# Earlier loads of the attention heads, a later chain for the outputs, and an inverse root on GpSimd

## Chip, core and metric

The kernel runs on one core of one Trainium2 chip, as one launch. The metric is the device time in microseconds, taken as the median over runs; lower is better. Engines are written as the profile has them: PE is TensorE, DVE is VectorE, ACT is ScalarE, POOL is GpSimd, SP is SyncE, which here does nothing but issue DMAs in a fixed order.

## What is computed

One transformer block on 2048 rows of 576 float32 numbers. The conditioning vector `c` gives, through SiLU and one product with `w_mod`, six rows: shift, scale and gate for each half of the block.

```python
h = layernorm(x) * (1 + ca) + sa
x = x + ga * (softmax_attention(h @ wqkv, 32 heads of 18) @ wo)
h = layernorm(x) * (1 + cb) + sb
x = x + gb * ((sigmoid(h @ w_gate) * (h @ w_up)) @ w_down)     # inner width 4608
layernorm(x) = (x - mean) / sqrt(var + 1e-5)
```

The scores' softmax runs over all 2048 keys. Products keep nearly float32 accuracy: operands are split into a high and a low part (`fp32r`), and the parts are multiplied separately.

## The kernel before

**Three stages.** First the rows are normalized, transposed and projected to q, k and v; the split parts of q and k go to DRAM (`qd`, `kd`). Then attention runs in 32 units of 16 steps. Last, the gated block runs with a Strassen-like scheme of seven products for each of 18 column blocks, twice (two halves of the rows).

**A unit of attention** is two heads and half of the queries. Units 0 to 15 take the first half of the queries, units 16 to 31 the second. A step `kt` (0 to 15) takes 128 keys: four score matmuls (line 916), four exponentials on ACT (line 920), and the product of earlier probabilities with v (`values`, line 539, two steps late, so that a pair of steps holds two groups of eight such matmul records). Beside them runs `maxima`, six steps and more ahead: it computes the scores of the next unit but one turned the other way (line 446) and takes their row maxima on DVE (line 452). At the end of a unit's maxima, which falls at step 9 of the unit before it, DVE makes `nm`, `turned` and `parts` (lines 464 to 469, the last two instructions are a cast and a subtraction of 128x32 in SBUF), and SP sends them through DRAM into rows of the q tile (lines 470 and 475). Most units pair two of the maxima's tiles by a ReLU on ACT; the units in `SINGLE` (0, 1, 16, 17, 18, 27, 28, 29) don't.

**Order of work.** During attention the order on PE, DVE and SP is the order of the program (`manual_schedule`); ACT and POOL follow a scheduler's order. A string of letters says what a step does: `t` scores, `m` one turn of the maxima, `v` values, `k` copies a finished unit's output out of PSUM (`taken`, the copy is `oT`, line 553), and `w` does one piece of side work. `k` and `w` are in odd steps alone. Each `w` takes the next entry of the list that `outputs` returned and the next piece of a generator: `first_rows` from step 240 (`FROM0`) on, `project_o(8, 16)` from `FROM1` on.

**`load_heads(u + 2)`** issues eight DMAs on SP that fetch q and k of the unit after next (1.5 MB, line 413 to 421). Before, it stands behind step 1 of unit u.

**`outputs`** divides a finished unit by its sums: `gather` (line 571) moves the sums across partitions by a DMA, `spread` takes the reciprocal on DVE (line 574), writes it to DRAM (`rows_r`, line 575) and reads it back broadcast (line 576); `scaled` multiplies and splits on POOL (lines 579 to 581, three instructions of 128x512); `stored` writes the result to `od` in DRAM (line 592). The list has one entry for each `w`, that is for steps 1, 3, 5 and so on of the next unit.

**`first_rows`** scales `wo` (`load_wo`, ending in a row of empty yields that wait for unit 15's outputs), multiplies the first eight row tiles with it (`project_o(0, 8)`), normalizes the result and makes the operands of the last stage. `load_o(t)` fetches row tile t of `od` (the tile `t`, lines 645 and 650) and the row of x (line 652). `project_o` calls it one tile ahead; a tile takes two `w` (line 676). Row tiles 8 to 15 go the same way in units 27 to 29.

**`ln_scales_steps`** turns variances into inverse roots: `var + 1e-5` on DVE (line 167), the root on ACT (line 169), then reciprocal and one Newton step on DVE (lines 172 to 177). It is called four times ahead of attention, once in attention (in unit 20, eight columns), and twice in the last stage. Between its yields `first_rows` puts one more.

Of the kernel before, what the change touches and what calls it, by code (L numbers as in the profile page):

```python
# [15 lines left out]
F32 = mybir.dt.float32  # L16
F32R = mybir.dt.float32r
AF = mybir.ActivationFunctionType
ALU = mybir.AluOpType
# [4 lines left out]
P = 128  # L24
# [10 lines left out]
EPS = 1e-5  # L35
# [2 lines left out]
HW = S // 2  # L38
UNITS = H
LEAD = 6  # L40
FROM0, FROM1 = 15 * 16, 27 * 16 + 13
DL = 384
ORDER = (1, 6, 2, 7, 5, 4, 3)
LOOK = 3
# [11 lines left out]
def tile_block(ctx, tc, x_in, wqkv, wo, w_gate, w_up, w_down, c_in, w_mod, out):  # L56
    nc = tc.nc
# [3 lines left out]
    const = ctx.enter_context(tc.tile_pool(name="const", bufs=1))  # L61
# [4 lines left out]

    ident = const.tile([P, P], F32, name="ident")
    make_identity(nc, ident)
    eps = const.tile([P, 1], F32, name="eps")
    nc.vector.memset(eps, EPS)  # L70
    mcol = const.tile([P, 2, 5], F32, name="mcol")
    mcol2 = const.tile([P, 2, 6], F32, name="mcol2")
    gb_b = const.tile([P, D], F32, name="gb_b")
# [85 lines left out]
    def ln_scales(pool, mv, rs):  # L159
        for _ in ln_scales_steps(pool, mv, rs):  # L160
            pass

    def ln_scales_steps(pool, mv, rs):

        n = rs.shape[-1]
        var = pool.tile([P, n], F32, name="var")
        nc.vector.tensor_scalar_add(var, mv[:, :, 1], EPS)
        sd = pool.tile([P, n], F32, name="sd")
        nc.scalar.activation(sd, var, AF.Sqrt)
        yield  # L170
        r0 = pool.tile([P, n], F32, name="r0")
        nc.vector.reciprocal(r0, sd)

        nc.vector.tensor_mul(sd, r0, r0)
        nc.vector.tensor_mul(sd, sd, var)
        nc.vector.tensor_scalar(sd, sd, -0.5, 1.5, op0=ALU.mult, op1=ALU.add)
        nc.vector.tensor_mul(rs, r0, sd)

    def ln_apply(z, xt, mean, rs):

# [208 lines left out]
    def temp(shape, dtype):  # L389
        temps["n"] += 1  # L390
        return qpool.tile(shape, dtype, name=f"t{temps['n'] % 2}")
# [8 lines left out]
    def heads(u):  # L400
        return qsets[u % 3], ksets[u if u < 2 else 2 + (u - 2) % 3]

    def load_heads(u):


        qs, ks = heads(u)
        half, p = divmod(u, H // 2)
        n = S if u < 2 else S + 512
        own = slice(half * HW, (half + 1) * HW)
        for h in range(2):  # L410
            rows = slice((2 * p + h) * DH, (2 * p + h + 1) * DH)
            two, one = (slice(64 * h + a, 64 * h + b) for a, b in ((0, 2 * DH), (2 * DH, 3 * DH)))
            nc.sync.dma_start(
                qs[two, :].bitcast(F32), qd[:, rows, own].rearrange("l f n -> f l n").bitcast(F32)
            )
            nc.sync.dma_start(qs[one, :].bitcast(F32), qd[0, rows, own].bitcast(F32))
            nc.sync.dma_start(
                ks[two, 0:n].bitcast(F32),
                kd[0, rows, 0:n].unsqueeze(1).to_broadcast([DH, 2, n]).bitcast(F32),
            )  # L420
            nc.sync.dma_start(ks[one, 0:n].bitcast(F32), kd[1, rows, 0:n].bitcast(F32))
# [72 lines left out]
    with tc.tile_pool(name="wv1", bufs=1) as wvp:  # L494
        tiles = [[(o + D * w, P)] for o in (128, 256, 384) for w in (0, 1)] + [[(DM, 64), (D + DM, 64)]]
        for i, parts in enumerate(tiles):
# [5 lines left out]
            for g in range(2):  # L502
                pl = project_qk([(wt, 2 * g), (wt, 2 * g + 1)], run if i else None)
                col, n = parts[-1]
# [43 lines left out]
    def taken():  # L548

        if "whole" in state:  # L550
            half, p, acc = state.pop("whole")
            oT = epool.tile([P, 512], F32, name="oT")
            nc.scalar.copy(oT, acc)
            todo_out.extend(outputs(half, p, oT))
# [3 lines left out]
    def outputs(half, p, oT):  # L558


        at = turns["out"] = (turns["out"] + 1) % 3
        if state["room"] is None:
            full, hi, lo = (ppool.tile([P, 512], F32, name=f"p{i}") for i in range(3))
        else:
            room = state["room"][:, 1536 * at : 1536 * (at + 1)]
            full, hi, lo = (room[:, 512 * i : 512 * (i + 1)] for i in range(3))
            parts = room[:, 512:1536]
        sums, rec = (epool.tile([P, 16], F32, name=n) for n in ("sums", "rec"))

        def gather():  # L570
            nc.sync.dma_start(sums, oT[DH::32, :].rearrange("j (q e) -> j q e", e=16))

        def spread():
            nc.vector.reciprocal(rec, sums)
            nc.sync.dma_start(rows_r.rearrange("j (q e) -> (j q) e", e=16), rec)
            nc.sync.dma_start(full, rows_r.unsqueeze(1).to_broadcast([4, 32, 512]))

        def scaled():
            nc.gpsimd.tensor_mul(full, full, oT)
            nc.gpsimd.tensor_copy(hi.bitcast(F32R), full)  # L580
            nc.gpsimd.tensor_sub(lo.bitcast(F32R), full, hi)

        def stored():
            for h in range(2):
                f0 = (2 * p + h) * DH
                for c in range(2):
                    q, q0 = 32 * (2 * h + c), half * HW + c * 512
                    if state["room"] is None:
                        for l, part in enumerate((hi, lo)):
                            nc.sync.dma_start(od[l, f0 : f0 + DH, q0 : q0 + 512].bitcast(F32), part[q : q + DH])  # L590
                        continue
                    nc.sync.dma_start(
                        od[:, f0 : f0 + DH, q0 : q0 + 512].rearrange("l f q -> f l q").bitcast(F32),
                        parts[q : q + DH].rearrange("f (l q) -> f l q", l=2),
                    )

        return [gather, spread, None, None, scaled, None, stored]

# [3 lines left out]
    def load_wo():  # L604

        wo_h = slots.tile([P, 4, 640], F32R, name="w0")[:, :, 0:D]
        wo_l = slots.tile([P, 4, 640], F32R, name="w1")[:, :, 0:D]
        we = bgp.tile([P, 2, D], F32R, name="we")
        raws = {}

        def load(t):
            raw = raws[t] = temp([P, 2048], F32)[:, 0:D]
            if t < 4:
                paced(nc.gpsimd.dma_start(raw, wo[t * P : (t + 1) * P, :]))
            else:
                for p0 in (0, 64):
                    paced(nc.gpsimd.dma_start(raw[p0 : p0 + 64], wo[DM:D, :]))

        load(0)
        yield  # L620
        load(1)
        yield
        for t in range(5):
            raw = raws[t]
            nc.gpsimd.tensor_mul(raw, raw, ga_b)
            wh, wl = (wo_h[:, t, :], wo_l[:, t, :]) if t < 4 else (we[:, 0, :], we[:, 1, :])
            nc.gpsimd.tensor_copy(wh, raw)
            nc.gpsimd.tensor_sub(wl, raw, wh.bitcast(F32))
            if t >= 3:
                for i, w in enumerate((wh, wl)):  # L630
                    nc.gpsimd.dma_start(wod[:, i, t - 3, :].bitcast(F32), w.bitcast(F32))
            if t < 3:
                load(t + 2)
            yield
        weights.extend((wo_h, wo_l, we))
        for _ in range(8):
            yield

    def load_o(t):
# [104 lines left out]

    def first_rows():
        yield from load_wo()
        yield from project_o(0, 8)
        for t in range(8):
            ln_stats(bgp, Oa[:, t, :], mv2[:, t, :])
            yield  # L750
        for _ in ln_scales_steps(bgp, mv2[:, 0:8, :], rs2[:, 0:8]):
            yield
            yield
# [49 lines left out]
    def paced(load):  # L803

        tc.add_manual_dep(
            load.ins, state["exp"].ins.name,
            mybir.DependencyInfo(mybir.DependencyClass.Sync, mybir.DependencyReason.DATA),
            reason="paced by the steps of attention",
        )
# [70 lines left out]
    for u in range(UNITS):  # L880
        half, p = divmod(u, H // 2)
        qs, ks = heads(u)
        if u == UNITS - 1:
            state["room"] = temp([P, 2048], F32)
            turns["out"] = 2
        if u == H // 2:
            state["room"] = big.tile([P, 8, 640], F32, name="big").rearrange("p a b -> p (a b)")
        for kt in range(NT):
# [30 lines left out]
                    pr = probs[2 * c + h] = ppool.tile([P, 512], F32, name=f"p{2 * c + h}")  # L919
                    state["exp"] = nc.scalar.activation(pr, sT, AF.Exp, scale=SCALE)  # L920
            pending.append((half, p, kt, probs))
            if 0 < u < UNITS - 2 and kt == 1:
                load_heads(u + 2)
            if u in (1, 3):
                if kt == 2:
                    a = big.tile([P, 8, 640], F32, name="big")
# [332 lines left out]
```

## Time and profile before

| | us |
|---|---|
| median of 3 runs | 2955.37 |
| lowest and highest | 2953.96, 2956.30 |
| the profiled execution's own time | 2952.37 |
| its span, first to last instruction | 2950.6 |
| PE busy | 2848.5 (97%) |
| DVE busy | 2215.6 (75%) |
| ACT busy | 1570.4 (53%) |
| POOL busy | 684.8 (23%) |

Attention lies between about 238 and 1611 us of the span; unit u has about 40 us, more where side work is done. A line of the timeline gives the start in the span, the duration, engine, source line, operation, output and input tiles and, in brackets, how long the engine had been idle and who ended that. A line of a window gives for each engine the busy time, and the share of its full clock that TensorE was granted (PEclk).

### The profile page before, as it was taken

What the parts mean: (1) busy time and instruction counts of PE and PEld (TensorE: products, weight loads), DVE (VectorE), ACT (ScalarE), POOL (GpSimd) and SP (SyncE); (2) the same over time, 40 slices, a digit from 0 to 9 for tenths busy, and PEclk for the clock granted to TensorE, in tenths of its full rate; (3) what the DMA queues carried; (4) which work ended last, traced back from release to release, by engine and by line L of the source; (5) the groups of instructions that cost most, each with busy time, mean ns of one, the idle gap of its engine ahead of it and who ended that gap; (6) DMA issues with size and microseconds to landing.
All of it is one profiled execution on the core that took longest, in us unless ns stands there. A gap on an engine that the chain in (4) does not pass through costs nothing.

```text
span 2950.6 us, 46231 instructions
## 1 busy us (share of the span) xinstructions
PE 2848.5 (97%) x16901; PEld 1876.0 (64%) x16901; DVE 2215.6 (75%) x4047; ACT 1570.4 (53%) x2908; POOL 684.8 (23%) x793
## 2 busy tenths in 40 slices
PE   7999999999999999999999899988999999999999
PEld 6863333333344534334443788877888888888888
DVE  7278889999999789999872778878877555555555
ACT  3217889999977688898678323333333111111111
POOL 3112025455221007730103322233222100000000
PEclk9999999999999999999999999999999999999999
DMA  5343244444223312321344776677555845545443
GB/s 178 123 160 87 65 125 156 155 144 135 88 79 92 109 54 92 111 74 59 101 132 153 273 239 228 234 256 249 207 200 211 321 159 176 170 167 167 165 157 136
DMA packets 177135, 456.26 MB, mean 155 GB/s; under 512 B 36488, under 2 KB 86412, under 8 KB 164620
## 3 DMA queue, kind: packets, MB, share of 16 engines
q1 hardware_dynamic: 162140, 376.72, 38.8%
q0 software_dynamic: 14768, 76.59, 7.4%
q8 instruction: 133, 2.18, 0.3%
q14 instruction: 94, 0.77, 0.1%
HBM read 285.07 MB, written 167.91 MB: 154 GB/s over the span
## 4 chain that ended last, share of the span: by engine, by line
PE 77%; DVE 11%; DMA 4%; issue 3%; ACT 3%; SPq 1%; POOL 1%; POOLq 0%; DVEq 0%; ACTq 0%
PE o L539 15%; PE d L1055 14%; PE x L1019 12%; PE s L446 10%; PE s L916 10%; PE bg L1019 4%; PE bu L1019 4%; DVE mx L452 4%; PE s L276 4%; PE s L327 2%; ACT p L920 2%; PE s L676 2%; DVE w L1011 1%; DMA xs<-ho 1%; DMA t<-od 1%
## 5 line engine op out<-in xcount | busy, mean ns | idle before, releaser
L452 DVE TENSOR_REDUCE mx<-s 128x1 f32<-128x512 f32 x1664 | 1057.3, 684 | 130.8 <-PE s L446 109.5
L920 ACT ACTIVATE p<-s 128x512 f32<-128x512 f32 x2048 | 1064.3, 611 | 165.6 <-PE s L916 80.8
L446 PE MATMUL s<-k,q 54*128 54x512 f32 x1920 | 610.4, 451 | 14.7 <-ACT p L920 6.3
L916 PE MATMUL s<-q,k 56*128 56x512 f32 x1920 | 559.0, 429 | 11.6 <-DVE mx L452 8.0
L539 PE MATMUL o<-p,vaug 128*32 128x512 f32 x4096 | 560.4, 612 | 0.4 <-ACT p L920 0.4
L1055 PE MATMUL d<-wd,hh 128*128 128x288 f32 x2304 | 475.5, 301 | 27.9 <-DVE Oa L1059 25.7
L446 PEld LDWEIGHTS s<-k,q 54*128 54x128 f32 x1920 | 278.2, 186 | 281.7 <-ACT p L920 225.1
L916 PEld LDWEIGHTS s<-q,k 56*128 56x128 f32 x1920 | 263.5, 187 | 300.1 <-DVE mx L452 216.1
L1055 PEld LDWEIGHTS d<-wd,hh 128*128 128x128 f32 x2304 | 378.4, 191 | 44.0 <-DVE Oa L1059 33.6
L1059 DVE TENSOR_TENSOR Oa<-Oa,d 128x288 f32<-128x288 f32 x576 | 256.0, 452 | 133.3 <-PE d L1055 129.0
L1055 PE MATMUL d<-wd,hl 128*128 128x288 f32 x1152 | 343.8, 298 | 0.0
L1019 PE MATMUL x<-k,w 128*128 128x512 f32 x1008 | 244.3, 393 | 4.2 <-ACT w L1010 4.2
L1055 PEld LDWEIGHTS d<-wd,hl 128*128 128x128 f32 x1152 | 220.1, 191 | 0.0
L1019 PEld LDWEIGHTS x<-k,w 128*128 128x128 f32 x1008 | 188.8, 190 | 43.8 <-ACT w L1010 5.6
L1031 ACT ACTIVATE u<-u 128x512 f32<-128x512 f32 x72 | 45.4, 631 | 320.2 <-DVE u L1207 316.2
L539 PEld LDWEIGHTS o<-p,vaug 128*32 128x32 f32 x4096 | 84.0, 108 | 167.7 <-issue 155.8
L1028 ACT ACTIVATE sg<-x 128x512 f32<-128x512 f32 x36 | 21.6, 599 | 315.7 <-PE x L1019 315.6
L1061 POOL DMA_DIRECT2D out_dram<-Oa x16 | 8.7, 544 | 604.3 <-DVE Oa L1059 604.3
L455 ACT ACTIVATE over<-s 128x512 f32<-128x512 f32 x192 | 114.6, 597 | 37.9 <-PE s L446 32.3
L457 DVE CUSTOM_DVE_ANT_0 over<-s,over 128x512 f32<-128x512 f32 x192 | 129.4, 674 | 0.0
L1019 PE MATMUL x<-big,w 128*128 128x512 f32 x504 | 120.5, 390 | 2.2 <-issue 2.2
L1019 PE MATMUL x<-w,w 128*128 128x512 f32 x504 | 121.2, 390 | 0.0
(211 smaller groups left out, 3555.0 us busy)
## 6 DMA issues: line engine op xcount, KB each, us to landing
ws<-w SPq DMA_DIRECT2D x126, 640.0 KB
w<-ws SPq DMA_DIRECT2D x126, 640.0 KB
wd<-wds SPq DMA_DIRECT2D x36, 1152.0 KB
k<-kd SPq DMA_DIRECT2D x60, 360.0 KB
wds<-w POOLq DMA_DIRECT2D x18, 1152.0 KB, 5.5
k<-kd SPq DMA_DIRECT2D x60, 180.0 KB
w<-in_B_w_down_dram POOLq DMA_DIRECT2D x18, 576.0 KB, 5.1
q<-qd SPq DMA_DIRECT2D x64, 144.0 KB
```

What stands on the lines that cost most here:

```text
L276: nc.tensor.matmul(acc, w, hT[:, t, cols], start=n == 0, stop=n == len(ts_) - 1)
L327: nc.tensor.matmul(acc[:, 0:HALF], hT[:, k, rows], w, start=n == 0, stop=n == len(ts_) - 1,)
L446: nc.tensor.matmul(sp, qs[rows, qt * P : (qt + 1) * P], ks[rows, at * 512 : (at + 1) * 512], start=True, stop=True,)
L452: nc.vector.tensor_reduce(to, sp, axis=AX.X, op=ALU.max)
L455: nc.scalar.activation(over, sp, AF.Relu)
L457: nc.vector.tensor_tensor_reduce(out=over, in0=sp, in1=over, scale=1.0, scalar=LOWEST, op0=ALU.add, op1=ALU.max, accum_out=mx[:, h * n + q ...
L539: nc.tensor.matmul(acc[32 * j : 32 * j + 32, :], vaug[:, kt, (2 * p + h) * VW : (2 * p + h) * VW + 32], probs[2 * c + h], start=kt == 0, s ...
L916: nc.tensor.matmul(sT, ks[rows, kcols], qs[rows, c * 512 : (c + 1) * 512], start=True, stop=True)
L920: state["exp"] = nc.scalar.activation(pr, sT, AF.Exp, scale=SCALE)
L1019: nc.tensor.matmul(acc[v], w[:, v, a, :], X[s][:, b, :], start=first and n == 0, stop=n == 6, skip_group_check=not first,)
L1055: nc.tensor.matmul(acc[:, :HALF], a[:, f, rows], w[:, f, cols], start=n == 0, stop=n == 5)
L1059: nc.vector.tensor_add(Oa[:, t, cols], Oa[:, t, cols], acc[:, :HALF])
```

## The change

`load_heads(u + 2)` moves from the end of step 1 to the front of step 0 of a unit, ahead of the previous unit's `gather` on SP. `spread` is cut in two: `inverted` (reciprocal and the write to DRAM) at step 7, `spread` (the read back) at step 9; `scaled` moves from step 9 to 13, `stored` from 13 to 15. So that it still follows `stored`, `load_wo` has nine empty yields instead of eight, and `FROM1` lies two steps later. The root on ACT and the reciprocal on DVE give way to one `pow` with exponent -0.5 on POOL and two Newton steps on DVE, with a yield behind each.

```diff
-FROM0, FROM1 = 15 * 16, 27 * 16 + 13
+FROM0, FROM1 = 15 * 16, 27 * 16 + 15
...
-    eps = const.tile([P, 1], F32, name="eps")
-    nc.vector.memset(eps, EPS)
+    powers = const.tile([P, 8], F32, name="powers")
+    nc.gpsimd.memset(powers, -0.5)
...
         var = pool.tile([P, n], F32, name="var")
+        sd = pool.tile([P, n], F32, name="sd")
+        r0 = pool.tile([P, n], F32, name="r0")
         nc.vector.tensor_scalar_add(var, mv[:, :, 1], EPS)
-        sd = pool.tile([P, n], F32, name="sd")
-        nc.scalar.activation(sd, var, AF.Sqrt)
+        nc.gpsimd.tensor_tensor(r0, var, powers[:, 0:n], op=ALU.pow)
         yield
-        r0 = pool.tile([P, n], F32, name="r0")
-        nc.vector.reciprocal(r0, sd)
-
-        nc.vector.tensor_mul(sd, r0, r0)
-        nc.vector.tensor_mul(sd, sd, var)
-        nc.vector.tensor_scalar(sd, sd, -0.5, 1.5, op0=ALU.mult, op1=ALU.add)
-        nc.vector.tensor_mul(rs, r0, sd)
+        for to in (r0, rs):
+            nc.vector.tensor_mul(sd, r0, r0)
+            nc.vector.tensor_mul(sd, sd, var)
+            nc.vector.tensor_scalar(sd, sd, -0.5, 1.5, op0=ALU.mult, op1=ALU.add)
+            nc.vector.tensor_mul(to, r0, sd)
+            yield
...
-        def spread():
+        def inverted():
             nc.vector.reciprocal(rec, sums)
             nc.sync.dma_start(rows_r.rearrange("j (q e) -> (j q) e", e=16), rec)
+
+        def spread():
             nc.sync.dma_start(full, rows_r.unsqueeze(1).to_broadcast([4, 32, 512]))
...
-        return [gather, spread, None, None, scaled, None, stored]
+        return [gather, None, None, inverted, spread, None, scaled, stored]
...
-        for _ in range(8):
+        for _ in range(9):
             yield
...
         qs, ks = heads(u)
+        if 0 < u < UNITS - 2:
+            load_heads(u + 2)
...
-            if 0 < u < UNITS - 2 and kt == 1:
-                load_heads(u + 2)
```

## The prediction

> **What bounds the kernel now.** I read the page first, then PE's idle time, then the timeline around each idle stretch in attention.
>
> ```profile
> span 2950.6 us, 46231 instructions
> PE 2848.5 (97%) x16901; PEld 1876.0 (64%) x16901; DVE 2215.6 (75%) x4047; ACT 1570.4 (53%) x2908; POOL 684.8 (23%) x793
> ```
>
> PE works for 97% of the span, so only some 100 us of idle time are to be had, and a stretch in which PE waits lengthens the whole. The change takes no matmul away. It is worth what it does to single stalls of PE in attention; three of them lie where the change works.
>
> The first is the root in unit 20. ACT's rows, PE's rows and one window (PEclk, the share of its clock that TensorE was granted, is the third figure from the end):
>
> ```profile
> 1091.25 1.28 ACT L169 ACT_TABLE_LOAD   x1
> 1092.78 1.28 ACT L920 ACT_TABLE_LOAD   x1
> ...
> 1090.25 1.07 PE L539 MATMUL o<-p,vaug 128*32 128x512 f32 x8
> 1094.72 0.79 PE L916 MATMUL s<-q,k 56*128 56x512 f32 x1 [2.50 <-ACT p L920]
> 1095.44 1.94 PE L539 MATMUL o<-p,vaug 128*32 128x512 f32 x8
> 1099.74 1.66 PE L539 MATMUL o<-p,vaug 128*32 128x512 f32 x8
> 1102.45 1.06 PE L539 MATMUL o<-p,vaug 128*32 128x512 f32 x8
> ...
> 1094.70:1099.70 5.00, 4.98 (x18) 1.99 (x18) 1.33 (x3) 3.43 (x8) 0.00 (x0) 0.50 0.60 191
> ```
>
> ACT loads the root's table, computes, loads the exponential's table back: 1091.25 to 1094.06, 2.81 us in which no exponential runs. PE stands for 2.50 us, and then the granted clock is 0.50 for 5 us: the same eight records take 1.94 us instead of 1.07. The groups should start 2.71 us apart (1099.74 to 1102.45); the two intervals from 1090.25 to 1099.74 are 9.49 us, so the stall cost 9.49 - 5.42 = 4.07 us, 1.57 us more than the idle time itself.
>
> The others are in units 28 and 29, where the projection waits for its tile of outputs:
>
> ```profile
> 1440.62 1.47 PE L676 MATMUL s<-w,t 128*128 128x288 f32 x9
> 1450.88 2.60 PE L676 MATMUL s<-w,t 128*128 128x288 f32 x9 [4.35 <-DMA t<-od]
> 1459.02 1.47 PE L676 MATMUL s<-w,t 128*128 128x288 f32 x9
> 1465.14 1.45 PE L676 MATMUL s<-w,t 128*128 128x288 f32 x9
> 1505.72 2.60 PE L676 MATMUL s<-w,t 128*128 128x288 f32 x9 [3.76 <-DMA t<-od]
> ...
> 1429.52 0.79 SPq L413 DMA_DIRECT2D q<-qd  x1
> 1435.90 0.36 SPq L575 DMA_DIRECT2D rows_r<-rec  x1
> 1442.78 0.60 SPq L576 DMA_DIRECT2D big<-rows_r  x1
> 1443.47 1.02 SPq L645 DMA_DIRECT2D t<-od  x2
> ```
>
> These pieces should be 6.12 us apart (1459.02 to 1465.14); 1440.62 to 1459.02 is 18.40, an excess of 6.16 us for 4.35 us of idle time. The second, by the same surcharge of 1.8 us, cost 3.76 + 1.8 = 5.6 us. SP's rows show why: the heads' loads go out from 1429.52, the small write of the reciprocals behind them (1435.90) lands only at 1442.78, SP stands still until then, and the tile's load is issued behind that, at 1443.47, for a matmul due at about 1446.7.
>
> **The change part by part.** The root: the pair of table loads in unit 20 goes, and no other row holds ACT there, so -4.1 us. The Trainium skill, ScalarE: Activation LUTs, section on what ACT_TABLE_LOAD costs, puts every switch of a set at about 2.66 us, half of it a drain; for two switches that makes an estimate of 5.3 us saved on ACT and about 6.6 in all. The trace shows 2.81 us for both, and the sum uses that.
>
> The heads first, the chain later. In unit 17 this does harm:
>
> ```profile
> 924.76 0.39 SPq L645 DMA_DIRECT2D t<-od  x1
> 927.79 1.07 PE L539 MATMUL o<-p,vaug 128*32 128x512 f32 x8
> 932.85 1.06 PE L539 MATMUL o<-p,vaug 128*32 128x512 f32 x8
> 936.65 1.85 PE L676 MATMUL s<-w,t 128*128 128x288 f32 x12
> ```
>
> The first tile of outputs was requested at 924.76, ahead of the unit, which begins at 932.85. With the ninth empty yield its request comes at step 1, behind the heads and the gather on SP, and it is used at step 3. A pair of steps without projection takes 5.06 us there (927.79 to 932.85); the first piece, at 936.65 before, is due one pair later, at 941.7. In this queue a transfer issued behind the heads landed 13.3 us after their start (1429.52 to 1442.78). For the tile itself I take 1.2 us more, between nothing and the 7.4 us from 1443.47 to the matmul at 1450.88, where two tiles came at once; near the low end, since it is fetched beside the heads' last transfers. The heads start at about 932.3, when unit 16 has read its last scores; the tile lands 14.5 us later, at 946.8. PE stands for 5.1 us and pays the surcharge of 1.8: +6.9 us. The ends: 13.3 us gives 3.9 of idle time, +5.7; 20.7 us gives 11.3, +13.
>
> In units 28 and 29 it does good: no `spread` stands between the heads and `load_o` any more. The tile used at step 5 is requested at step 1. Two pieces of 6.12 us ahead of 1440.62 step 1 has its piece, at 1428.4; the unit begins 3.8 us before that (932.85 to 936.65), at 1424.6; the tile lands at 1439.1, 1.5 us before the piece that needs it. Both stalls go: -6.2 - 5.6 = -11.8 us.
>
> The next part is a collision. DVE's two small instructions at the end of a unit's maxima stand still while POOL works on SBUF:
>
> ```profile
> L468 DVE CAST parts<-turned 128x32 fp32r<-128x32 f32 x32 | 12.3, 384 | 1.1
> L469 DVE TENSOR_TENSOR parts<-turned,parts 128x32 fp32r<-128x32 f32 x32 | 11.4, 356 | 1.1
> 1241.82 2.61 POOL L723 TENSOR_TENSOR ho<-t,ho 32x512 fp32r<-32x512 f32 x2
> 1243.17 1.30 DVE L469 TENSOR_TENSOR parts<-turned,parts 128x32 fp32r<-128x32 f32 x1
> 1245.13 0.50 PE L916 MATMUL s<-q,k 56*128 56x512 f32 x1 [1.29 <-DVE mx L452]
> ...
> 813.29 0.24 DVE L574 RECIPROCAL rec<-sums 128x16 f32<-128x16 f32 x1
> 829.73 0.18 DVE L468 CAST parts<-turned 128x32 fp32r<-128x32 f32 x1
> 829.94 0.19 DVE L469 TENSOR_TENSOR parts<-turned,parts 128x32 fp32r<-128x32 f32 x1
> 813.26 1.07 PE L539 MATMUL o<-p,vaug 128*32 128x512 f32 x8
> 822.99 1.07 PE L539 MATMUL o<-p,vaug 128*32 128x512 f32 x8
> 821.23 0.59 SPq L576 DMA_DIRECT2D Oa<-rows_r  x1
> 826.11 1.29 POOL L579 TENSOR_TENSOR Oa<-Oa,oT 128x512 f32<-128x512 f32 x1 [36.23 <-DMA Oa<-rows_r]
> 1543.70 0.34 SPq L575 DMA_DIRECT2D rows_r<-rec  x1
> 1545.13 0.57 SPq L576 DMA_DIRECT2D big<-rows_r  x1
> ```
>
> The subtraction that takes 0.19 us alone took 1.30, until POOL's second instruction ended at 1244.43, and PE then stood for 1.29 us. Against 0.18 and 0.19 us the two groups hold (12.3 - 5.8) + (11.4 - 6.1) = 11.8 us of this now. The change places `scaled` anew in every unit. In unit 14 the reciprocal moves two pairs of steps later, 9.73 us (813.26 to 822.99), from 813.29 to 823.0; it runs 0.24 us, its write takes 1.43 to the read back in a quiet queue (1543.70 to 1545.13), and that 4.88 to the multiplication (821.23 to 826.11): `scaled` would start at 829.6, within 0.2 us of the cast at 829.73. So small a margin is a coin toss, unit by unit. All present collisions gone would be -11.8; one of 1.2 us in each of 26 units (without 17, 18, 28 and 29, where the projection gives DVE time) 31 - 11.8 = +19. I take +2: half of the units now quiet are hit, and some of the present ones go.
>
> The rule that speaks against this change is in the Trainium skill, SBUF — State Buffer, section on the two separate sides: VectorE and GpSimd share a port pair under an exclusive lock, and the loser blocks for the other's whole instruction. The rows at 1241.82 and 1243.17 agree; its result is the slower rival below.
>
> Last, the power and the longer Newton. Three DVE instructions more of at most 0.19 us are +0.5 us in unit 20, taken in full.
>
> ```profile
> 11.21 1.71 POOL L184 COPY x<-x 128x64 f32<-128x64 f32 x4 [1.62 <-DVE x L181]
> 17.73 0.77 PE L192 MATMUL s<-ident,x 128*128 128x128 f32 x5
> 1795.01 0.63 ACT L1031 ACTIVATE u<-u 128x512 f32<-128x512 f32 x1 [5.51 <-DVE u L1207]
> ```
>
> No row shows a power on POOL. Its product of 128x512 takes 1.29 us; eight columns are a 64th of that, so 1.29 us is also the price if each power costs as much as 64 products. I take that, the geometric middle of the ends: 0.19, what DVE needs for so small a tile, and 12.9, ten times my value. DVE reads it two `w`, four steps or 10.8 us (twice 5.42), later, so unit 20 hides all but the upper end; past that, the maxima queued behind the Newton step on DVE wait, and PE with them. Ahead of attention the cover is 4.8 us, from the end of POOL's copies (12.92) to PE's transposes (17.73): nothing at my value, up to +8 at the end. In the last stage ACT, behind the root's loads, waited 5.51 us for DVE anyway, so their removal brings nothing; a slow power there would hold the additions queued behind it on DVE by up to 12.9 us.
>
> Sum: -4.1 + 0.5 - 11.8 + 6.9 + 2 = -6.5 us. The profiled execution's own time is 2952.37 (span 2950.6 and 1.8 around it), 3.0 below the median of 2955.37; 2945.9 there is 2948.9 as a median.
>
> **The rivals.** *No stall in unit 17* (the tile overtakes the heads): -13.4 us, 2942. For it: no row shows a large transfer behind the heads; against: the small write at 1435.90, which didn't overtake them. *POOL's port decides*: `scaled` starts ahead of the subtraction in nearly all units, +19 instead of +2, 2966, slower; it decides from a start less than about 0.2 us behind the cast's. *The stalls of units 28 and 29 stay*, since the margin there is 1.5 us: without the -11.8, 2961; for it, the 7.4 us tile. *A slow power*, at its end of 12.9 us: +8 ahead of attention and +2 in unit 20 instead of nothing, 2959.
>
> **How the numbers follow.** Forecast 42%, no stall in unit 17 20%, POOL's port 20%, stalls stay 10%, slow power 8%. 0.2%, about what a measurement can tell here, is 5.9 us: faster is under 2949.5, slower over 2961.3. The forecast's own range is 2942 to 2956, so somewhat over half of it is faster: with the second case 0.45. Slower gets 0.14 of POOL's port, half of the stalls and some of the slow power: 0.21; the rest, 0.34, is the same. The range 2939 to 2965 leaves out the worst of POOL's port and of unit 17's upper end.
>
> **What would show it.** Right: no table load in attention; groups of line 539 in unit 20 without a gap; no idle time of line 676 in units 28 and 29; one of 4 to 6 us at step 3 of unit 17, with a clock of 0.50 behind it; lines 468 and 469 at a sum near 24 us. Wrong: that sum above 35 us, a gap of line 676 in unit 28, POOL's power above 5 us, or DVE waiting for it.

## The result, and the profile after

The changed kernel takes 2968.46 us in the median of five runs (2963.11 to 2972.41), the kernel before 2953.98 us of five (2951.38 to 2956.30): a ratio of 1.0047, 95% interval 1.0032 to 1.0061. It is 14 us slower. Forecast were 2948.9 us and at most 2965.

The head of the page after:

```profile
span 2961.2 us, 46269 instructions
PE 2851.4 (96%) x16901; PEld 1878.1 (63%) x16901; DVE 2222.5 (75%) x4067; ACT 1558.7 (53%) x2894; POOL 695.2 (23%) x801
```

The profiled execution is the fastest of the five, so it shows 10.6 us of the loss and not all of it. This table gives the span by stretches, worked out from the first value matmul (line 539) of each unit; "quiet" is the edit of e5 and e6 below, e15 and e16 are the last two experiments.

| us | before | changed | before, quiet | changed, quiet | e15 | e16 |
|---|---|---|---|---|---|---|
| to the first row | 238.0 | 245.4 | 242.6 | 244.7 | 238.9 | 240.4 |
| units 0 to 14 | 610.9 | 617.9 | 611.8 | 614.3 | 615.1 | 612.0 |
| 15, 16 | 90.5 | 83.1 | 88.7 | 82.4 | 83.7 | 84.0 |
| 17, 18 | 106.4 | 117.7 | 105.9 | 114.3 | 105.8 | 106.4 |
| 19, 20 | 92.0 | 87.5 | 93.6 | 85.6 | 86.5 | 86.2 |
| 21 to 27 | 293.3 | 295.0 | 287.5 | 289.5 | 289.1 | 288.1 |
| 28, 29 | 107.6 | 98.1 | 108.1 | 96.0 | 96.2 | 96.0 |
| 30, 31 | 68.5 | 75.8 | 68.5 | 76.3 | 68.5 | 68.5 |
| behind attention | 1343.6 | 1340.8 | 1338.3 | 1344.2 | 1341.7 | 1341.6 |
| span | 2950.6 | 2961.2 | 2945.0 | 2947.3 | 2925.5 | 2923.1 |

**What came as forecast.** In the changed kernel's timeline the tiles of units 28 and 29 are there when they are due (no brackets, so no idle time), and in unit 17 PE stands for 4.85 us (5.1 forecast), with a granted clock of 0.50 in the window behind it. SP's rows show the heads' loads from 940.18 and the tile's request only behind them:

```profile
1450.36 1.47 PE L678 MATMUL s<-w,t 128*128 128x288 f32 x9
1505.71 1.46 PE L678 MATMUL s<-w,t 128*128 128x288 f32 x9
...
940.18 0.81 SPq L413 DMA_DIRECT2D q<-qd  x1
946.40 0.99 SPq L647 DMA_DIRECT2D t<-od  x1
955.12 2.19 PE L678 MATMUL s<-w,t 128*128 128x288 f32 x6 [4.85 <-DMA t<-od]
955.00:960.00 5.00, 4.84 (x18) 3.91 (x18) 0.46 (x2) 0.00 (x0) 0.00 (x0) 0.50 0.67 189
```

**What nobody had forecast: unit 30.** The same read back that left SP free earlier in units 28 and 29 now comes three pairs later, and the first loads of the last stage (`raw`) stand right behind it on SP. The write of the maxima comes behind them:

```profile
1561.01 0.57 SPq L578 DMA_DIRECT2D big<-rows_r  x1
...
1563.62 0.93 SPq L855 DMA_DIRECT2D raw<-in_B_w_up_dram  x1
1566.49 3.22 SPq L470 DMA_DIRECT2D rows_m<-parts  x1
1578.83 2.87 SPq L475 DMA_DIRECT2D q<-rows_m  x4
1583.11 1.19 PE L920 MATMUL s<-q,k 56*128 56x512 f32 x3 [5.65 <-DMA q<-rows_m]
```

SP's rows of the kernel before, for the same place:

```profile
1547.44 0.56 SPq L853 DMA_DIRECT2D raw<-in_B_w_up_dram  x1
1560.36 0.34 SPq L470 DMA_DIRECT2D rows_m<-parts  x1
1564.90 3.16 SPq L475 DMA_DIRECT2D q<-rows_m  x4
```

There the last of the loads went out 13 us ahead of the maxima's write, and 4.5 us lay between the write and its read back. Now it is 2.9 us and 12.3, and PE stands for 5.65 us.

**The start.** The power took 1.05 us, less than the 1.29 taken. But look at which DVE instruction stands between the two Newton steps:

```profile
9.61 1.05 POOL L170 TENSOR_TENSOR r<-var,powers 128x4 f32<-128x4 f32 x1
10.69 0.16 DVE L173 TENSOR_TENSOR sd<-r 128x4 f32<-128x4 f32 x1 [1.37 <-POOL r L170]
11.29 0.16 DVE L176 TENSOR_TENSOR r<-r,sd 128x4 f32<-128x4 f32 x1
20.54 0.42 DVE L134 COPY mrow<-s 128x256 f32<-128x256 f32 x1 [9.09 <-PE s L121]
20.89 0.15 DVE L173 TENSOR_TENSOR sd<-r 128x4 f32<-128x4 f32 x1
...
22.12 2.04 DVE L181 TENSOR_SCALAR x<-x,mv,rs 128x576 f32<-128x576 f32 x4
22.75 1.54 PE L192 MATMUL s<-ident,x 128*128 128x128 f32 x6 [0.75 <-DVE x L181]
```

Outside attention the order on DVE is the scheduler's. It put the copy of the modulation's rows, which waits 9.09 us for PE, ahead of the second step. The kernel before, whose PE began its transposes at 17.73:

```profile
10.57 2.05 DVE L181 TENSOR_SCALAR x<-x,mv,rs 128x576 f32<-128x576 f32 x4
```

x is normalized at 22.12 instead of 10.57, and PE's transposes come 5 us later.

**The last stage.** Two of the seven powers stand there, and the forecast gave them no price. DVE stands still until POOL has finished each of them, the additions queued behind on DVE come later, and PE waits for those: 1.20 us at the first (1802.09) and 1.32 at the second, whose rows are these:

```profile
1875.71 1.01 POOL L170 TENSOR_TENSOR r<-var,powers 128x4 f32<-128x4 f32 x1
1876.76 0.16 DVE L173 TENSOR_TENSOR sd<-r 128x4 f32<-128x4 f32 x1 [1.36 <-POOL r L170]
1877.34 0.54 PE L1057 MATMUL d<-wd,hh 128*128 128x288 f32 x2 [1.32 <-DVE Oa L1061]
```

All fifteen traces with the power in the last stage have both stops, 2.4 to 2.7 us together; in the three with the root there (before, e2, e6) PE has no idle time at these places. Behind attention the fifteen take 1343.4 us in the mean, the three 1340.4.

**The collisions.** The groups of the cast and the subtraction at the end of a unit's maxima (busy time, mean ns), 29.1 us instead of 23.7:

```profile
L469 DVE TENSOR_TENSOR parts<-turned,parts 128x32 fp32r<-128x32 f32 x32 | 16.5, 515 | 1.1
L468 DVE CAST parts<-turned 128x32 fp32r<-128x32 f32 x32 | 12.6, 395 | 1.3 <-DVE turned L466 0.2
```

One of them, in unit 5, in rows of DVE, POOL and PE, and two windows behind it:

```profile
478.86 0.76 DVE L468 CAST parts<-turned 128x32 fp32r<-128x32 f32 x1
479.65 0.73 DVE L469 TENSOR_TENSOR parts<-turned,parts 128x32 fp32r<-128x32 f32 x1
478.79 1.54 POOL L834 TENSOR_TENSOR w<-w 128x288 fp32r<-128x288 f32 x2
481.04 0.50 PE L920 MATMUL s<-q,k 56*128 56x512 f32 x1 [0.84 <-DVE mx L452]
482.00:484.00 2.00, 1.89 (x10) 0.63 (x12) 2.00 (x6) 2.00 (x5) 2.00 (x4) 0.84 0.01 2
484.00:486.00 2.00, 2.00 (x12) 0.83 (x6) 0.78 (x4) 0.26 (x2) 1.68 (x3) 0.50 0.38 137
```

The two instructions need 0.18 and 0.19 us alone. They lost 1.1 us here, PE stood for 0.84, and the granted clock fell to 0.50, so that the next step took 3.71 us instead of 2.14. That surcharge is not certain: in units 5 to 13 of before, the changed kernel and e1 to e4, 12 steps at this place took 3.85 us or more (2.74 is the usual), and behind four of them the next step took 3.55 to 3.71.

In unit 5 DVE meets the preparation of weights (line 834), work that stands where it stood in the program. From unit 13 on it meets `scaled` in its new place. Unit 27, in rows of POOL, DVE and PE:

```profile
1424.20 1.29 POOL L581 TENSOR_TENSOR big<-big,oT 128x512 f32<-128x512 f32 x1 [38.38 <-DMA big<-rows_r]
1424.81 0.72 DVE L468 CAST parts<-turned 128x32 fp32r<-128x32 f32 x1
1425.56 0.65 DVE L469 TENSOR_TENSOR parts<-turned,parts 128x32 fp32r<-128x32 f32 x1
1426.86 0.50 PE L920 MATMUL s<-q,k 56*128 56x512 f32 x1 [0.69 <-DVE mx L452]
```

Of the 64 casts and subtractions of this trace, 32 took more than 0.30 us. By the POOL instruction that each overlaps most, 19 of them, in twelve units from 13 to 29, met `scaled` and lost 11.4 us; 13, in units 5 to 12, met line 834 and lost 5.6. In the kernel before 26 took as long: 6 met `scaled` (3.5 us), 13 the preparation of weights (3.6) and 7 other work (4.5).

### The profile page after: what moved, and what is told of

Same layout as the page of the kernel before. It is cut to its first block, busy times and chain, and to the rows that moved or that the text cites. A ratio compares the mean times of both kernels' runs of the same rounds, so it can differ in the third digit from the quotient of the medians.

```text
span 2961.2 us, 46269 instructions
## 1 busy us (share of the span) xinstructions
PE 2851.4 (96%) x16901; PEld 1878.1 (63%) x16901; DVE 2222.5 (75%) x4067; ACT 1558.7 (53%) x2894; POOL 695.2 (23%) x801
```

## The experiments

Each diff shows the part of the edit that matters, against the changed kernel unless another is named.

The first theory (A) was that the separate places of the table add up. Its rival (B) was the collisions alone.

**e1**: the power alone; order, chain and yields as before. Against the kernel before:

```diff
-        nc.scalar.activation(sd, var, AF.Sqrt)
+        nc.gpsimd.tensor_tensor(r0, var, powers[:, 0:n], op=ALU.pow)
```

> The changed normalization alone (power and two Newton steps); the order of the heads' loads and the outputs' chain are those of before. Theory A, several places with prices of their own add up: the stretch before the first row of attention starts 5 to 8 us later (the second Newton step of x's mean and variance stands behind the copy of mrow on VectorE), unit 20 gives 4 us back, units 15 to 18 and 28 to 30 are those of before; sum 0 to +4 us against before. Theory B, the loss is VectorE blocked by GpSimd in attention: this kernel has the old place of the chain, so it has none of it, and with unit 20's gain it is 4 us faster than before.

2961.52 us, ratio to before 1.0024 (1.0011 to 1.0037). The first row came at 246.5, unit 20 took 41.2 us instead of 47.4: 6.2 us, more than the 4.1 of the forecast. But one unit, 21, took 50.1 instead of 40.5. DVE's, POOL's and PE's rows there:

```profile
1166.05 6.20 DVE L468 CAST parts<-turned 128x32 fp32r<-128x32 f32 x1
1165.92 1.26 POOL L718 TENSOR_TENSOR ho<-t,ho 128x512 fp32r<-128x512 f32 x1
1167.13 0.60 POOL L716 CAST t<-t 128x512 fp32r<-128x512 f32 x1
1167.69 0.79 POOL L719 DMA_DIRECT2D xs<-ho  x1
1168.50 1.27 POOL L727 TENSOR_TENSOR t<-t 128x512 f32<-128x512 f32 x1
1169.72 1.26 POOL L718 TENSOR_TENSOR t<-t,t 128x512 fp32r<-128x512 f32 x1
1170.94 1.26 POOL L727 TENSOR_TENSOR t<-t 128x512 f32<-128x512 f32 x1
1173.46 0.79 PE L916 MATMUL s<-q,k 56*128 56x512 f32 x1 [6.08 <-DVE mx L452]
```

A cast of 0.18 us stood through five instructions of POOL and the issue of a DMA between them, which followed one another without idle time. The order of attention is that of before, with a start 8.5 us later; there this run of POOL's pieces didn't meet the end of the maxima.

**e2**: heads first and later chain alone, root on ACT, one Newton step.

```diff
-        nc.gpsimd.tensor_tensor(r0, var, powers[:, 0:n], op=ALU.pow)
+        nc.scalar.activation(sd, var, AF.Sqrt)
```

> The heads' loads first and the later chain alone; the normalization keeps ScalarE's square root and one Newton step. Theory A: the start of attention is that of before, unit 17 loses 8 to 9 us, unit 30 loses 7, the reciprocal at the chain's fourth step 0.2 us in each unit, units 28 and 29 gain 9 to 10 and units 15 and 16 some 7; together +3 to +10 us against before, with unit 20's table loads still there. Theory B: all of the loss of the changed kernel and more, +14 to +18 us, since the square root's 4 us in unit 20 are not given back.

2976.28 us, 1.0077 (1.0056 to 1.0098): more than either theory gave. The first row came at 242.1, units 17 and 18 took 116.5, 28 and 29 98.0, 30 44.8, all as A has it; but units 7, 10 and 14 had the surcharge of the clock, and in unit 22 the cast and the subtraction stood for 6.68 and 3.52 us.

**e3**: 8 yields.

```diff
-        for _ in range(9):
+        for _ in range(8):
```

> The changed kernel with 8 instead of 9 empty steps at the end of the loading of wo, so that the first tile of the row stage asks for the data of unit 14's outputs one step later against them. Theory A: the stop of TensorE at the third row of unit 17 (4.85 us of idle time and the low clock behind it) goes, 7 to 9 us less than the changed kernel, if the whole row stage then runs one step later and no other collision moves in. Theory B (collisions alone): the stop is no more than a place where the collisions of units 17 and 18 show; the time stays within 3 us of the changed kernel.

2973.21 us, 1.0068 (1.0046 to 1.0090): no gain against the changed kernel's 1.0047. Yet the stop of unit 17 was gone, units 17 and 18 took 106.6 instead of 117.7; unit 21 took 52.9 instead of 42.2, with 6.65 and 3.52 us for the two instructions, nearly as in e2's unit 22.

**e4**: the old root ahead of attention (what `True` asks for), the power inside it and behind it.

```diff
-            ln_scales(ln, mv, rs)
+            ln_scales(ln, mv, rs, True)
```

> The changed kernel with ScalarE's square root, the reciprocal and one Newton step in the four normalizations ahead of attention, and the power with two steps only inside it. Theory A: the first row of attention starts 6 to 8 us earlier than in the changed kernel and the whole is as much faster, about level with or 2 to 5 us above before by median against median. Theory B: the start is hidden behind the loads of the weights and the time is within 2 us of the changed kernel.

2969.30 us, 1.0051 (1.0032 to 1.0069), not faster than the changed kernel, though the first row came at 240.3. Unit 13 took 42.9 us (40.1 in the quiet kernel e5) by a collision with the clock's surcharge. So theory A fell as it stood: each place answered as it should, and the sum didn't. Theory C took its place: the collisions are a term of their own, every shift throws them anew, and they cover the rest.

**e5, e6**: the transposed maxima in PSUM, in the changed kernel and in the kernel before.

```diff
-            turned = small.tile([P, 32], F32, name="turned", bufs=1)
+            turned = sp[:, 0:32]
```

> The changed kernel with one edit: the transposed maxima are written into the first 32 columns of the last score tile in PSUM instead of a tile in SBUF, so that VectorE's cast and subtraction at the end of a unit's maxima read PSUM. Theory C: these two stand still only because they have their operands in SBUF while GpSimd works there, and TensorE pays the stop and at times a half-speed stretch behind it. Then lines 468 and 469 take about 12 us in all units together instead of 29, and the kernel is 8 to 14 us faster than the changed kernel (12 to 17 of collisions beyond 0.37 us a unit, part of it hidden), the spread of its runs is smaller. Theory D: any instruction of VectorE that writes SBUF waits for GpSimd; then lines 468 and 469 stay near 29 us and so does the time.

> The kernel before with the same single edit (the transposed maxima in PSUM). Theory C: the collisions at the ends of units 15, 16 and 6 to 9 go, 11.9 us of them on VectorE: 6 to 12 us faster than before. Theory D: no change within 2 us. The difference of the changed kernel to before without collisions (this run against the changed kernel with the same edit) is by theory A still +5 to +15 us: start 6, unit 17 8 to 9, unit 30 7, reciprocal 6, against 4 in unit 20 and 9 to 10 in units 28 and 29.

The changed kernel takes 2949.91 us, ratio to before 0.9987 (0.9977 to 0.9996), the kernel before 2946.22, 0.9985 (0.9975 to 0.9994). e5's groups:

```profile
L468 DVE CAST parts<-s 128x32 fp32r<-128x32 f32 x32 | 6.1, 191 | 1.1
L469 DVE TENSOR_TENSOR parts<-s,parts 128x32 fp32r<-128x32 f32 x32 | 6.1, 191 | 1.1
```

12.2 us instead of 29.1, and units 6 to 13 are 40.07 to 40.09 us each, where they had been 40.15 to 40.62. The edit was worth 0.0060 of 2954 us, 17.7, to the changed kernel (1.0047 to 0.9987) and 0.0015, 4.4 us, to the one before (the medians say 18.6 and 7.0). So some 13 of the 14 us of loss are collisions, with an uncertainty of some 6 us by the intervals. The traces agree: in the table, span less start less the part behind attention, the edit makes attention shorter by 16.6 us in the changed kernel (1375.0 to 1358.4) and by 4.9 in the one before (1369.0 to 1364.1). Without the collisions the two ratios lie 0.0002 apart, 0.6 us, with intervals of 3 us each (the medians differ by 3.7): the other gains and losses of the change cancel. In a unit with few collisions the edit itself costs 0.1 to 0.4 us (39.85 in e6 against 39.5 to 39.8 in units 9 to 13 before), perhaps because the last score tile comes free later; no run shows why. The two instructions still write SBUF and no longer wait, so theory D falls. The Trainium skill, SBUF — State Buffer, section on the two separate sides, says that a VectorE instruction in a two-port mode or with two operands in SBUF contends with GpSimd for a shared pair of ports; that PSUM takes these two out of it agrees.

**e7**: the old chain for the last two units.

```diff
+        if half * (H // 2) + p >= 29:
+            return [gather, lambda: (inverted(), spread()), None, None, scaled, None, stored]
```

> The changed kernel, but the outputs of units 29 and 30 go by the chain of before (reciprocal, write and read back at its second step). Theory A: in unit 30 the loads of the last stage's rows go out behind a read back at step 3 again, well ahead of the write of the maxima; the stop of 5.65 us there goes and unit 30 takes about 36 us instead of 43, 7 us less in all. Theory E: the stop comes from the order of the heads' loads and stays.

2962.87 us, 1.0036 (1.0024 to 1.0049). Unit 30 took 39.8, neither 36 nor 43: the stop at the maxima was gone, but another came at step 3. e8 shows it in DVE's row.

**e8**: a selection. Heads first only in units 28 and 29, late chain only for the outputs of 27 and 28, 8 yields, with e4's and e5's edits.

```diff
+        if half * (H // 2) + p not in (27, 28):
+            return [gather, lambda: (inverted(), spread()), None, None, scaled, None, stored]
```

> A selection: heads' loads first and the late chain only around units 28 and 29 (outputs of units 27 and 28), everything else in the order of before with 8 empty steps; square root by ScalarE ahead of attention, power inside it; transposed maxima in PSUM. Theory A with C: start as before, no reciprocal in the way, no stop in units 17, 20, 28, 29 and 30, no collisions: 4 + 9 + 7 to 10 us faster than before, 2930 to 2937. If the gains of units 28 and 29 need the new order in all units, 2939 to 2945.

2937.22 us, 0.9950 (0.9935 to 0.9965), just over the upper edge. Unit 30 lost 6 us: the reciprocal waits on DVE for the gather.

```profile
1525.14 0.25 DVE L587 RECIPROCAL rec<-sums 128x16 f32<-128x16 f32 x1 [2.89 <-DMA sums<-oT]
```

e11 below was planned on the belief that unit 28's late stores hold that gather up. The trace speaks for something else: those stores went out at 1500.93 and the gather at 1516.32, and from 1514 to 1524 the DMA engines were busy throughout (share 1.00 to 1.10), in which time POOL had transfers of 1280 KB each under way for the last stage, issued from 1511.76 on.

**e9, e10, e11**: e4's, e3's and a better edit for unit 30, each on the quiet changed kernel of e5. e11's:

```diff
+        if half * (H // 2) + p >= 29:
+            return [gather, None, lambda: (inverted(), spread()), None, scaled, None, stored]
```

> The changed kernel with the transposed maxima in PSUM, so that the collisions no longer cover other differences (2949.9 us), and with ScalarE's square root, reciprocal and one Newton step in the normalizations ahead of attention. If the power's place on VectorE's queue ahead of attention costs what the traces so far suggest (the first row at 245.1 us in the mean of five traces with it, at 241.0 in the mean of five without), the first row starts at 239 to 243 us and the whole takes 2944 to 2948. If the start doesn't set the end, 2948 to 2952.

> The changed kernel with the transposed maxima in PSUM and 8 instead of 9 empty steps. Theory A: the stop at the third row of unit 17 goes, units 17 and 18 take 106 us together instead of 114.3, the whole 2941 to 2945; no large stop moves to units 21 or 22, since the collisions are gone. Rival: one step earlier means a new stop elsewhere, and the time stays at 2948 to 2952.

> The changed kernel with the transposed maxima in PSUM; the outputs of units 29 and 30 have their reciprocal, write and read back at the third step of the chain, not at its second, where VectorE waited 2.9 us for the gather behind unit 28's late stores. Theory A: no stop at the write of the maxima, none at the gather, unit 30 takes 36 us instead of 43.8, the whole 2941 to 2944. If the raw loads a pair of steps later than before still stand ahead of that write, unit 30 stays above 38.

e9: 2948.37 us, 0.9972 (0.9962 to 0.9982), first row at 240.5. Against e5 that is -1.5 us by the medians and -4.4 by the ratios, whose intervals overlap; the time alone doesn't settle it. The place of the first row does: 242.3 to 246.5, mean 245.0, in nine traces of kernels with the power ahead of attention, 238.0 to 242.6, mean 240.8, in nine with the root. e10: 2942.73, 0.9950 (0.9935 to 0.9965), units 17 and 18 105.9 instead of 114.3, as theory A gave. e11: 2939.07, 0.9942 (0.9927 to 0.9958), unit 30 35.65 instead of 43.8 and the whole 2 us faster than expected.

**e12**: e8 with the third-step chain for unit 29, and the late chain for unit 14 too. In part:

```diff
+        if u not in (14, 27, 28):
```

> The selection with two edits more: unit 29's chain with its reciprocal, write and read back at the third step, and the late chain for unit 14 too, so that GpSimd reads unit 14's outputs ahead of the last part of wo and ScalarE's copy of unit 15's doesn't wait for it. Theory A: unit 30 36 us instead of 42.1, units 15 and 16 82 to 84 us instead of 87.1; 2926 to 2931 in all. If unit 14's multiplication isn't moved ahead by its later chain, 2930 to 2934.

2932.44 us, 0.9917 (0.9902 to 0.9931). Unit 30 was mended (35.6), units 15 and 16 got worse, 90.1. What stops PE at the end of unit 15 is seen in e6, in rows of POOL, ACT and PE:

```profile
894.58 1.26 POOL L579 TENSOR_TENSOR Oa<-Oa,oT 128x512 f32<-128x512 f32 x1
895.87 0.58 ACT L553 COPY oT<-o 128x512 f32<-128x512 f32 x1 [1.89 <-POOL Oa L579]
897.01 0.49 PE L916 MATMUL s<-q,k 56*128 56x512 f32 x1 [2.04 <-ACT p L920]
```

ACT's copy of unit 15's output waits until POOL has read unit 14's, which stands behind the parts of `wo` in POOL's queue; a later chain made that later still.

**e13, e14**: on e5 with the power. e13 has the heads first, the old chain and 8 yields; e14 the late chain, 9 yields and the heads at their old place. e13's edit, in part:

```diff
-        return [gather, None, None, inverted, spread, None, scaled, stored]
+        return [gather, lambda: (inverted(), spread()), None, None, scaled, None, stored]
```

> Maxima in PSUM, the changed normalization, the heads' loads first in a unit; the chain, the start of the last rows' loading and the 8 empty steps of before. As the prediction argued (a read back behind the heads in SP's queue holds SP up), the stops of units 28 and 29 stay, since the read back still stands between the heads and the tile; and the gather, now behind the heads, lands after the reciprocal's turn at the third step: VectorE waits some 3 us for it in most units, TensorE with it, 1 to 4 us in each of 25 units, 2975 to 3030 in all. If the gather isn't held up by the heads, the time is 2945 to 2955 with units 28 and 29 at 108 together.

> Maxima in PSUM, the changed normalization, the late chain with its 9 empty steps; the heads' loads behind the second step as before. If the later chain alone takes the stops of units 28 and 29 away (no read back in front of the tile's load on SP), units 28 and 29 take 96 us together, the reciprocal still costs 0.22 us a unit, unit 30 still stops, and the time is 2943 to 2953. If the heads' place does it, 28 and 29 stay at 108 and the time is 2955 to 2965.

e13: 3064.76 us, 1.0385 (1.0366 to 1.0403). The group of reciprocals shows it, 113 us of waiting:

```profile
L574 DVE RECIPROCAL rec<-sums 128x16 f32<-128x16 f32 x32 | 8.1, 253 | 113.1 <-DMA sums<-oT 112.9
```

Units 28 and 29 took 96.8 nevertheless, against what was expected: so the read back at step 3 isn't by itself what holds the tile up. SP's rows of unit 28 show why:

```profile
1531.85 0.81 SPq L413 DMA_DIRECT2D q<-qd  x1
1546.77 0.36 SPq L575 DMA_DIRECT2D rows_r<-rec  x1
1548.20 0.58 SPq L578 DMA_DIRECT2D big<-rows_r  x1
```

The write comes 14.9 us behind the heads' start, where it came 6.4 behind in the prediction's rows (1429.52 to 1435.90), and the read back follows it after 1.4 us instead of 6.9: the heads' transfers no longer stand in front of it.

e14: 2948.70, 0.9981 (0.9972 to 0.9991), units 28 and 29 95.9: the late chain does it alone, and heads first aren't needed for it. Units 5 to 14 took 399.3 us, as in e6 (399.2) and not as in e5 (401.5), so the late reciprocal, which I had charged with 0.22 us a unit, costs nothing that shows. ACT's rows of unit 8, of e14:

```profile
594.46 4.21 ACT L922 ACTIVATE p<-s 128x512 f32<-128x512 f32 x8
```

and of e5:

```profile
595.56 3.07 ACT L924 ACTIVATE p<-s 128x512 f32<-128x512 f32 x6
```

Between two of the maxima's ReLUs e14 and before have 8 exponentials; e5, e2 and the changed kernel have 10 ahead of one ReLU and 6 ahead of the next. ACT's order is the scheduler's, and it is the heads' place that makes it another: e13, with the heads first and the old chain, has a 10 and a 6 too, a little earlier in the unit. All traces without collisions fit, e13 with its waits aside: units 5 to 14 take 399.1 to 399.3 us with 8 throughout and 401.5 to 401.7 with 10 and 6. No run changed ACT's order alone, so that it costs these 2.3 us is likely but not shown.

**e15, e16**: all causes known by then removed, once with the changed order in all units (e15), once with e12's selection without unit 14 and with the row stage two steps later (e16). e16's edit against e12, in part:

```diff
-FROM0, FROM1 = 15 * 16, 27 * 16 + 15
+FROM0, FROM1 = 15 * 16 + 2, 27 * 16 + 15
...
-        for _ in range(8):
+        for _ in range(7):
```

> The changed order in all units with every cause found so far removed: maxima in PSUM, 8 empty steps, unit 29's and 30's chain with the read back at its third step, square root ahead of attention. If the causes add up: 2939.1 of the run with unit 30 mended, less 7 for units 17 and 18, less 2 to 4 for the start: 2927 to 2931. If they cover one another: 2932 to 2939.

> The second selection without the late chain for unit 14; instead the row stage starts two steps later (FROM0) with one empty step less, so that GpSimd's multiplication of unit 14's outputs comes ahead of the last part of wo, and the tiles are requested as before. If ScalarE's copy waited for that multiplication, units 15 and 16 take 82 to 84 us instead of 90.1 and the whole 2924 to 2928; if the loading of wo is only shifted against it, 2930 to 2934.

e15: 2930.85 us, 0.9929 (0.9911 to 0.9947); the causes add up. e16: 2928.17, 0.9916 (0.9901 to 0.9932), 25 us faster than the kernel before, the fastest of all, and within 0.2 us of the 2924 to 2928 expected. Units 15 and 16 took 84.0. From the head of its page:

```profile
PE 2825.2 (97%) x16901; PEld 1863.1 (64%) x16901; DVE 2205.0 (75%) x4055; ACT 1562.4 (53%) x2899; POOL 691.3 (24%) x797
```

PE has the same 16901 matmuls in 26 us less busy time than in the changed kernel: what is gone is in part the stretches at half clock, for the mean granted clock of the profiled executions rose from 0.988 to 0.994. The two powers of the last stage are still there.

## Why the prediction was wrong

**The collisions, +2 us, are the step that failed.** The mechanism was named and its rival, POOL's port, was priced at +19 instead of +2 and 2966 us; 2968.5 was measured. That the rival came so near is partly luck: its 19 was too much, and the terms beside it came out worse than it had them. Mis-sized was the term: against before it measures about 13 us.

That `scaled` might meet the cast was foreseen, and it did so in twelve units, eight of them not hit before; four of these eight (17, 18, 28 and 29) the prediction had left out. But the term nets new hits against old ones by DVE's time alone, and there it comes out near: DVE's two groups went from 23.7 to 29.1 us, +5.4. A hit's time on DVE isn't its price. Taking the hits away saves DVE 11.5 us in the kernel before and gains 4.4 (7.0 by the medians); in the changed kernel it saves 16.9 and gains 17.7. One reason is the clock's surcharge of 1.5 us at times, which the term left out, though the prediction charged a like one at every stop; what else makes up the difference is open. The term also took one hit for one instruction of POOL, 1.2 us, where a run of POOL's pieces can hold DVE for 6 to 10 us; units 21 and 22 of e1 to e3 had that, the profiled run of the changed kernel didn't. The criterion for being wrong, a sum of lines 468 and 469 over 35 us, was therefore too wide: 29.1 in that trace was already a loss.

**Unit 30, +7.8 us (76.3 against 68.5, quiet), was not in the sum.** The prediction followed the read back past the heads and the tile, but not what else stands behind it on SP: in unit 30 the raw loads, and behind them the maxima's write.

**The start, some +4 us, was held to be covered.** The power was rightly sized. What failed is the cover of 4.8 us: it counted the power's duration on DVE's chain, not that a second Newton step in a stretch without a fixed order can be put behind a waiting copy. (The geometric middle of the ends 0.19 and 12.9 is 1.57 us and not 1.29; no term hangs on it, since 1.0 to 1.7 was measured.)

**The last stage, +2.5 us, was put at nothing.** The prediction saw that a slow power would hold the additions behind it on DVE, but charged that to its upper end alone. A power of 1.0 to 1.4 us is enough: DVE waits 0.95 and 1.36 us for POOL, one of the signs of being wrong that the prediction had named, and PE stands for 1.20 and 1.32.

**ScalarE's order, likely +2.3 us in units 5 to 14, was not in the sum;** nor was the gain of 6.3 us in units 15 and 16, where ACT no longer waits for POOL (e6 has the wait of 1.89 us, e5 none).

**Right:** no table load in attention and -4.1 us for the root, which was too small: quiet, unit 20 gains 6.2 (47.5 to 41.2). The intervals of 2.71 us against which the stall was held were themselves stretched; e1 has 2.13 and 2.74 there. The Trainium skill, ScalarE: Activation LUTs, section on what ACT_TABLE_LOAD costs, from whose figure the prediction had worked out an estimate of 6.6, lay nearer, though the two loads themselves took 2.81 us on ACT and the prediction's rows show no drain around them, so that is partly luck. The stops of units 28 and 29, -11.8 forecast and -12.1 measured quiet, though not for the reason given alone: e13 and e14 show that the heads' place and the chain's each do it. Unit 17, +6.9 forecast and +8.4 measured. The three main terms give -9.0 as forecast and -9.9 as measured, so the quiet parts of the change that the prediction priced were right; those that it didn't see, 7.8 + 4.2 + 2.5 + 2.3 - 6.3 = 10.5, cancel them (e5 is 0.6 us slower than e6 by the ratios, 3.7 by the medians), and the collisions decided.

## What to carry to other kernels

Where two engines get into each other's way, an edit that moves the work of one also moves its meetings with the other, some systematically (here `scaled` onto the cast) and some by chance, and its time is that of its own effect plus these. Take the coupling away first (here one operand moved to PSUM), and then measure edits against that quiet kernel. When a wait is moved in a queue, list every unit's instructions behind it, the ones of the next stage too. And an edit in a hand-ordered stretch can still change an engine whose order is a scheduler's.

## What the runs showed of the hardware

In e1 a cast of 0.18 us on VectorE stood for 6.20 us through five instructions of GpSimd that followed one another, and through the issue of a DMA between them: the wait doesn't end with the first of them. With the transposed maxima in PSUM (e5, e6) the cast and the subtraction took 191 ns each in the mean, and none of them more than 0.30 us. A power of 128x4 or 128x8 on GpSimd took 1.0 to 1.7 us. In the changed kernel a stop of TensorE of 0.84 us was followed by a granted clock of 0.50 for 2.6 us or more (0.84 and 0.50 in the windows from 482 to 486); eight of the twelve longest steps at that place, in six kernels, were followed by one of the usual length.
